# Attention with memory, then a gated feed-forward layer, on one core: another order of work around each full pair's values

## The chip, the cores and the metric

The kernel is one program on one core of a Trainium2 chip. Its time is the device time of one execution in microseconds (us). A run is repeated, and the median of the runs is what counts. One more execution is taken with the hardware profiler, and all rows below come from that one. The core has four engines that compute: TensorE (PE, with its weight loads shown as PEld), VectorE (DVE), ScalarE (ACT) and GpSimd (POOL). SyncE (SP) issues most of the transfers. Each engine works through its own list of instructions in the order in which the program has them.

## The reference

```python
# q, k, v: (B=4, H=8, S=576, D=64); M_prev: (4, 8, 64, 64); z_prev: (4, 8, 64); beta: (8,)
scores = scale * np.matmul(q, k.transpose(0, 1, 3, 2))        # scale = 1/8
scores = np.where(causal, -1000000000.0, scores)
a = np.exp(scores - scores.max(-1, keepdims=True))
a /= a.sum(-1, keepdims=True) + 1e-09
local = np.matmul(a, v)
q_p = np.where(q > 0, q, np.exp(q) - 1.0) + 1.0
mem_ret = np.einsum('bhsd,bhde->bhse', q_p, M_prev)
mem_norm = np.einsum('bhsd,bhd->bhs', q_p, z_prev)[..., None] + 1e-06
g = 1.0 / (1.0 + np.exp(-beta))[None, :, None, None]
x = g * mem_ret / mem_norm + (1 - g) * local                  # -> (2304 tokens, 512)
h = x @ w_in                                                  # w_in (512, 2048)
out = (h * (1.0 / (1.0 + np.exp(-1.702 * h)))) @ w_out        # w_out (2048, 512)
```

## The kernel before

The work falls into three stages. In the first, up to about 100 us, the weights `w_in` are decoded and the first batch's attention is done. In the second, up to about 400 us, come the other three batches: 12 pairs of heads, each a "full pair". In the third the rest of the first matrix product and then the second matrix product run without attention.

The first matrix product is cut into 8 chunks of 256 or 320 tokens and 16 blocks of 128 columns, which makes 128 products. Each is 12 matmuls into one PSUM bank named `pm` (float values are split in a high and a low part, so three matmuls for each of four slices). There are two such banks while attention runs. ACT copies a finished bank out as `hk` (`gate`, line 981 stores it), and only then can the bank take another product. In the second stage these products fill TensorE's time between the parts of a pair.

One full pair does the following:

- `first_group`: scores of the fourth block of 128 rows, for two heads (tiles `ps`, 128x512). DVE takes the row maxima with the mask (`max_unit`, line 634, one custom instruction and a read of its accumulator, which lands in `nm`), ACT takes the exponentials with their sums (`exp_unit`, line 640), DVE adds and inverts the sums (lines 720 and 721), POOL scales the rows (line 643), and DVE transposes them in blocks of 32 into `eT` (`a_blocks`, line 847).
- `second_group`: the same for the third, second and first block of rows, in four banks named `rows`. These are the banks in which the values of the pair before stood (`po`), so the group waits until those have been read.
- `early_values`: the scores of the next pair's last 64 rows (`s_tail`), then the first half of the values in four banks `po`: the memory's part (`qpt`, `mr`) and the keys from block 8 on. The second half (keys 0 to 7) stands in `values["next"]` and is taken up by the next pair's `first_group`, ahead of its own scores.
- `x_sums` reads the values: ACT copies them as the high part `xh`, DVE subtracts to get the low part `xl`.
- Beside it POOL, ACT and DVE make the next pair's query features (`plan_prep`: `qmt`, `qp`, `nrm`), and `decode` turns the raw words of `w_out` into floats: one scaling on ACT (line 1085, `r<-wraw`) and three integer operations on DVE (lines 1067 to 1070).

The order is written by slots. `at(slot, prio, fn)` puts a piece of work in a slot, and within a slot the lower priority number comes first. A full pair takes eight slots from its `k0`. After the pieces of a slot `step` fills up with matmuls of the first matrix product, until a pace of 2.3 us of counted TensorE time per slot is reached:

```python
fill["debt"] += next(v for t, v in PACE if s < t) - (state["pe"] - t0)
while fill["debt"] > 0:
    r = next(fill["gen"], None)
```

A scheduler then orders each engine's list. `tc.add_manual_dep(..., NOSYNC, ...)` forces an order within one engine without a wait on the chip. With SYNC it is a wait.

## Time and profile before

| | us |
|---|---|
| median of 3 runs | 656.95 (653.60 to 657.05) |
| the profiled execution | 652.16 |
| its span, first to last instruction | 650.4 |
| PE busy | 562.4 |
| DVE busy | 424.6 |
| ACT busy | 341.4 |
| POOL busy | 250.4 |

The busy times are sums over stages that differ. The second stage is the one in which TensorE pauses. The rows below show that stage and one full pair of it, from the end of one pair's scores of the fourth rows to the end of the next pair's.

### The profile page before, as it was taken

What the parts mean: (1) busy time and instruction counts of PE and PEld (TensorE: products, weight loads), DVE (VectorE), ACT (ScalarE), POOL (GpSimd) and SP (SyncE); (2) the same over time, 40 slices, a digit from 0 to 9 for tenths busy, and PEclk for the clock granted to TensorE, in tenths of its full rate; (3) what the DMA queues carried; (4) which work ended last, traced back from release to release, by engine and by line L of the source; (5) the groups of instructions that cost most, each with busy time, mean ns of one, the idle gap of its engine ahead of it and who ended that gap; (6) DMA issues with size and microseconds to landing.
All of it is one profiled execution on the core that took longest, in us unless ns stands there. A gap on an engine that the chain in (4) does not pass through costs nothing. (4 is left out here: it accounts for less than half of the span.)

```text
span 650.4 us, 17377 instructions
## 1 busy us (share of the span) xinstructions
PE 562.4 (86%) x6984; PEld 497.4 (76%) x6984; DVE 424.6 (65%) x993; ACT 341.4 (52%) x816; POOL 250.4 (38%) x326
## 2 busy tenths in 40 slices
PE   5799898778768777787777877999999999999997
PEld 3377676556657666576665667999999999999997
DVE  5887875556656646476465473676649778856964
ACT  6687874334344344253353452475576775586442
POOL 4766586346356343463454533221041310230000
PEclk9599999888888897899989998999999999999999
DMA  7975445545544454454533435532274560472002
GB/s 253 372 254 188 126 141 162 177 126 160 177 129 150 150 167 129 134 171 156 176 131 131 133 110 182 204 111 94 92 253 120 177 190 15 135 242 96 24 1 74
DMA packets 48737, 97.74 MB, mean 150 GB/s; under 512 B 5520, under 2 KB 33424, under 8 KB 48656
## 3 DMA queue, kind: packets, MB, share of 16 engines
q1 hardware_dynamic: 42416, 74.60, 35.3%
q0 software_dynamic: 6240, 22.02, 10.9%
q8 instruction: 55, 0.90, 0.6%
q14 instruction: 26, 0.21, 0.1%
HBM read 73.01 MB, written 23.59 MB: 149 GB/s over the span
## 5 line engine op out<-in xcount | busy, mean ns | idle before, releaser
L141 PE MATMUL pm<-xh,wi 128*128 128x320 f32 (+1 forms) x1024 | 222.9, 312 | 43.0 <-ACT hk L160 39.2
L141 PEld LDWEIGHTS pm<-xh,wi 128*128 128x128 f32 x1024 | 171.6, 197 | 66.9 <-ACT hk L160 44.8
L1235 PE MATMUL acc<-oh,wo 128*128 128x384 f32 x672 | 169.7, 337 | 0.0
L141 PE MATMUL pm<-xl,wi 128*128 128x256 f32 (+1 forms) x512 | 154.9, 303 | 0.0
L1235 PEld LDWEIGHTS acc<-oh,wo 128*128 128x128 f32 x672 | 121.9, 188 | 0.0
L1235 PE MATMUL acc<-ol,wo 128*128 128x384 f32 x336 | 111.2, 337 | 0.0
L168 DVE TENSOR_TENSOR ol<-g,oh 128x768 fp32r<-128x768 f32 x84 | 79.8, 955 | 42.8 <-ACT oh L160 42.6
L643 POOL TENSOR_SCALAR a<-a,sm,g 128x512 f32<-128x512 f32 (+3 forms) x112 | 74.6, 676 | 69.9 <-DVE sm L721 59.3
L141 PEld LDWEIGHTS pm<-xl,wi 128*128 128x128 f32 x512 | 101.2, 198 | 0.0
L160 ACT ACTIVATE oh<-g 128x768 fp32r<-128x768 f32 x84 | 69.8, 841 | 46.7 <-PE acc L1235 35.8
L1178 POOL DMA_DIRECT2D g<-gd x48 | 34.8, 726 | 115.0 <-DVE ol L168 90.6
L141 PE MATMUL po<-eT,vr 32*64 32x64 f32 (+4 forms) x3072 | 52.9, 257 | 23.5 <-issue 23.5
L160 ACT ACTIVATE hk<-pm 128x256 f32<-128x256 f32 (+1 forms) x113 | 44.8, 410 | 49.8 <-PE pm L141 27.2
L141 PEld LDWEIGHTS po<-eT,vr 32*64 32x64 f32 x3072 | 47.2, 135 | 26.8 <-issue 26.7
L1235 PEld LDWEIGHTS acc<-ol,wo 128*128 128x128 f32 x336 | 62.9, 188 | 0.0
L640 ACT ACTIVATE a<-rows,nm 128x256 f32<-128x256 f32 (+1 forms) x72 | 33.2, 471 | 33.3 <-DVE nm L634 33.3
L847 DVE STREAM_TRANSPOSE eT<-a 128x1024 f32<-128x1024 f32 (+3 forms) x48 | 40.4, 842 | 14.1 <-POOL a L643 12.2
L640 ACT ACTIVATE a<-ps,nm 128x512 f32<-128x512 f32 (+1 forms) x40 | 26.5, 666 | 42.9 <-DVE nm L634 42.9
L1184 ACT ACTIVATE g<-g 128x768 f32<-128x768 f32 x48 | 39.6, 840 | 14.6 <-DMA g<-gd 14.3
L634 DVE CUSTOM_DVE_ANT_0 ps<-ps,mask 128x512 f32<-128x512 f32 (+3 forms) x72 | 38.2, 558 | 13.1 <-PE ps L141 12.1
L168 DVE TENSOR_TENSOR g<-g,g 128x768 f32<-128x768 f32 x48 | 45.4, 952 | 1.4 <-ACT g L1184 1.4
L168 POOL TENSOR_TENSOR qp<-qp,nrm 128x576 f32<-128x576 f32 (+1 forms) x16 | 17.2, 1072 | 75.0 <-DVE nrm L588 74.7
(146 smaller groups left out, 763.8 us busy)
## 6 DMA issues: line engine op xcount, KB each, us to landing
g<-gd POOLq DMA_DIRECT2D x48, 384.0 KB, 4.6
vr<-in_vt_dram SPq DMA_DIRECT2D x24, 576.0 KB, 4.2
gd<-hk SPq DMA_DIRECT2D x64, 160.0 KB, 2.7
kqf<-in_kq_dram SPq DMA_DIRECT2D x12, 768.0 KB, 4.7
wraw<-in_w_in_dram SPq DMA_DIRECT2D x16, 512.0 KB, 5.5
gd<-hk SPq DMA_DIRECT2D x64, 128.0 KB, 2.1
wraw<-in_w_out_dram SPq DMA_DIRECT2D x10, 512.0 KB, 3.5
qr<-in_qt_dram SPq DMA_DIRECT2D x12, 288.0 KB, 3.1
```

Of the source, the lines that this page charges most:

```text
L141: x = nc.tensor.matmul(out, l, r, start=start, stop=stop)
L160: return nc.scalar.activation(out=dst, in_=src, func=AF.Copy, **kw)
L168: return (nc.vector if eng == "V" else nc.gpsimd).tensor_tensor(out=dst, in0=a, in1=b, op=op)
L634: nc.vector.tensor_tensor_reduce(out=ps, in0=ps, in1=mk, op0=ALU.add, op1=ALU.min, scale=-0.125, scalar=1e38 if j == 0 else nm[:, j - 1:j] ...
L640: return nc.scalar.activation(out=a, in_=ps, func=AF.Exp, scale=-1.0, bias=nm, accum_out=sm)
L643: return (nc.vector if eng == "V" else nc.gpsimd).tensor_scalar(out=a, in0=a, scalar1=r, scalar2=gcol, op0=ALU.mult, op1=ALU.mult)
L847: x = nc.vector.transpose(out=blocks()[:, :4 * i + 4, i:9 - i:8 - 2 * i].rearrange("p k h n -> p h k n"), in_=U["a", i].rearrange("p h (k ...
L1178: x = nc.gpsimd.dma_start(t, gd[4 * kh + p][:, :, t0:t0 + QN].rearrange("i p t -> p i t"))
L1184: x = nc.scalar.activation(out=t, in_=t, func=AF.Gelu_apprx_sigmoid)
L1235: nc.tensor.matmul(acc[b, j][:, :QN], W[2 * p + kk][:, WPART[i], sp, 128 * j:128 * j + 128], mv[:, kk], start=first and p + kk == 0 and sp ...
```

## The change

- The second group stands one slot earlier, and one whole product of the first matrix product is put directly ahead of it and one directly behind it (`feed`, which goes on until a product is finished).
- One whole product is put behind the first half of the values, before the next pair's `first_group` takes the second half.
- `x_sums` leaves the subtractions to a new piece `x_rests`, one slot later and ordered behind the fourth rows' maxima of the next pair.
- In the second group the exponentials of the first and second rows get priorities behind the copies `hk`, those of the third rows stay ahead. `behind_hk` orders these exponentials and the pieces of `plan_prep` behind the last `hk`.
- `decode` loads seven slots later, so that its scaling and its integer operations fall under the values, and the integer operations are ordered behind the latest maxima instead of behind `xl`.

```diff
+    def behind_hk(x):
+        if "turn" in late_ps:
+            tc.add_manual_dep(x.ins, state["hk"], NOSYNC, reason="not yet")
...
             for x in xs:
                 tc.add_manual_dep(x.ins, state["exp"], NOSYNC, reason="not yet")
+                behind_hk(x)
...
+            if i < 2:
+                behind_hk(x)
             U["exp", h, i] = state["exp"] = state["late A"] = x.ins.name
...
-            for xl, src, xh in subs:
-                values["po"] = values["x"] = tt("V", xl, src, xh, ALU.subtract).ins.name
+
+        def x_rests():
+            for xl, src, xh in U["subs"]:
+                x = tt("V", xl, src, xh, ALU.subtract)
+                tc.add_manual_dep(x.ins, state["max"], NOSYNC, reason="not yet")
+                values["po"] = values["x"] = x.ins.name
             late_ps.pop("po").close()
...
-        at(k0 + 4, 20, second_group)
-        for i, k in ((3, 0), (2, 4), (1, 4), (0, 4)):
+        at(k0 + 3, 18, lambda: feed(1.0, True))
+        at(k0 + 3, 20, second_group)
+        at(k0 + 3, 22, lambda: feed(1.0, True))
+        for i, k in ((3, 0), (2, 3), (1, 3), (0, 3)):
+            x = k0 + k + 1
             for h in range(2):
                 at(k0 + k + 1, 13 - i, lambda h=h, i=i: max_unit(h, i))
-                at(k0 + k + 1, 28 - i, lambda h=h, i=i: exp_unit(h, i))
-                at(k0 + k + 2, 13 - i, lambda h=h, i=i: scale_unit(h, i))
+                at(x, (30, 29, 26, 25)[i], lambda h=h, i=i: exp_unit(h, i))
+                at(x + 1, 13 - i, lambda h=h, i=i: scale_unit(h, i))
...
         at(k0 + 7, 40, early_values)
+        at(k0 + 7, 99, lambda: feed(1.0, True))
...
+        at(k0 + 9, 15, x_rests)
...
+    def feed(us, whole=False):
+        end, done = state["pe"] + us, not whole
+        while (state["pe"] < end or not done) and fill["gen"] is not None:
+            gates = state["gates"]
+            r = next(fill["gen"], None)
+            if r is None:
+                fill["gen"] = None
+            done = not whole or state["gates"] > gates
+            if r:
+                return
...
+        def bits():
+            tc.add_manual_dep(bit_ops(raw, words, words).ins, last_max[0], NOSYNC, reason="not yet")
...
-        at(K0[MB * NP + 2 + i] - 4, 58, lambda i=i: decode(i))
+        at(K0[MB * NP + 2 + i] + 3, 58, lambda i=i: decode(i))
```

The order that results is shown for the pair of the rows below (the ninth full pair). First TensorE between the two halves of the values. `po` are the values, the rows with 64x32 are the last of the first half, those with 64x160 the first of the second. Before:

```order
L141 MATMUL po<-eT,vr 64x32 x4
L141 MATMUL po<-eT,vr 64x64
L141 MATMUL po<-eT,vr 64x32 x6
L141 MATMUL po<-eT,vr 64x160
L141 MATMUL po<-eT,vr 64x128
L141 MATMUL po<-eT,vr 64x160
L141 MATMUL po<-eT,vr 64x128 x2
```

Now:

```order
L141 MATMUL po<-eT,vr 64x32 x4
L141 MATMUL po<-eT,vr 64x64
L141 MATMUL po<-eT,vr 64x32 x6
L141 MATMUL pm<-xh,wi_524 128x320 x2
L141 MATMUL pm<-xl,wi_524 128x320
L141 MATMUL pm<-xh,wi_524 128x320 x2
L141 MATMUL pm<-xl,wi_524 128x320
L141 MATMUL pm<-xh,wi_524 128x320 x2
L141 MATMUL pm<-xl,wi_524 128x320
L141 MATMUL pm<-xh,wi_524 128x320 x2
L141 MATMUL pm<-xl,wi_524 128x320
L141 MATMUL po<-eT,vr 64x160
```

One product of 12 matmuls (block 524 of the program's names) has moved in between the halves.

Next DVE from the values to the scores' maxima. `eT<-at` is the transposition of the last 64 rows, `ps` with 128x512 are the fourth rows' maxima, `xl` the subtractions, `r` the integer operations of the decoding. Before:

```order
L856 STREAM_TRANSPOSE eT<-at 128x2x32
L168 TENSOR_TENSOR xl<-po,xh 128x256 x2
L168 TENSOR_TENSOR xl<-po,xh 64x64 x2
L855 STREAM_TRANSPOSE eT<-at 128x16x32
L586 TENSOR_REDUCE nrm<-qmt 128x9
L588 RECIPROCAL nrm<-nrm 128x9
L634 ISA ps,nm<-ps,mask 128x512
L634 ISA nm 128x1
L634 ISA ps,nm<-ps,mask 128x512
L634 ISA nm 128x1
```

Now:

```order
L1102 TENSOR_SCALAR r<-r 128x512
L1103 SCALAR_TENSOR_TENSOR r<-wraw,r 128x512
L1105 SCALAR_TENSOR_TENSOR r<-wraw,r 128x512
L869 STREAM_TRANSPOSE eT<-at 128x2x32
L642 ISA ps,nm<-ps,mask 128x512
L642 ISA nm 128x1
L642 ISA ps,nm<-ps,mask 128x512
L642 ISA nm 128x1
L168 TENSOR_TENSOR xl<-po,xh 128x256 x2
L168 TENSOR_TENSOR xl<-po,xh 64x64 x2
L868 STREAM_TRANSPOSE eT<-at 128x16x32
L592 TENSOR_REDUCE nrm<-qmt 128x9
```

The integer operations stood behind the maxima and now stand ahead of them. The subtractions, the long transposition and `nrm` stood ahead of the maxima and now stand behind.

A little further on DVE, from `nrm` to the second group's maxima (`rows`), the changed kernel has two orders. In six of the twelve pairs, the ninth among them, the transposition of the fourth rows (128x2x16x32) stands ahead of the second group's maxima, as it did before:

```order
L594 RECIPROCAL nrm<-nrm 128x9
L733 RECIPROCAL sm<-sm 128x2
L612 STREAM_TRANSPOSE qpt_4648<-qp 128x9x2x32
L860 STREAM_TRANSPOSE eT<-a_4531 128x2x16x32
L642 ISA rows,nm<-rows,mask 128x384
L642 ISA nm 128x1
L642 ISA rows,nm<-rows,mask 128x384
L642 ISA nm 128x1
```

In the six others, the eighth pair among them, it stands behind two or more of them:

```order
L594 RECIPROCAL nrm<-nrm 128x9
L733 RECIPROCAL sm<-sm 128x2
L612 STREAM_TRANSPOSE qpt_4264<-qp 128x9x2x32
L642 ISA rows,nm<-rows,mask 128x384
L642 ISA nm 128x1
L642 ISA rows,nm<-rows,mask 128x384
L642 ISA nm 128x1
L860 STREAM_TRANSPOSE eT<-a_4148 128x2x16x32
```

Nothing but the place of that transposition, and in some pairs that of `qpt`, differs between the two.

Last ACT from the fourth rows' exponentials (128x512) to the copies behind the second group. Before:

```order
L640 ACTIVATE a_4515,sum_162<-ps,nm 128x512 x2
L1085 ACTIVATE r<-wraw 128x512
L160 ACTIVATE mr<-mr,g 128x2x64 x2
L160 ACTIVATE hk<-pm 128x320 x3
L640 ACTIVATE a_4636,sum_163<-rows,nm 128x384 x2
L640 ACTIVATE a_4639,sum_164<-rows,nm 128x256
L640 ACTIVATE a_4639,sum_165<-rows,nm 128x128
L640 ACTIVATE a_4639,sum_164<-rows,nm 128x256
L640 ACTIVATE a_4639,sum_165<-rows,nm 128x128
L557 ACTIVATE qmt<-qr 128x9x64
L160 ACTIVATE hk<-pm 128x320 x2
L563 ACTIVATE qmt<-qmt 128x9x64
```

Now, from the copy of the product between the halves on:

```order
L160 ACTIVATE hk<-pm 128x320
L1120 ACTIVATE r<-wraw 128x512
L160 ACTIVATE xh<-po 128x256 x2
L160 ACTIVATE xh<-po 64x64 x2
L649 ACTIVATE a_4531,sum_162<-ps,nm 128x512 x2
L160 ACTIVATE mr<-mr,g 128x2x64 x2
L160 ACTIVATE hk<-pm 128x320 x2
L649 ACTIVATE a_4631,sum_163<-rows,nm 128x384 x2
L160 ACTIVATE hk<-pm 128x320
L649 ACTIVATE a_4643,sum_164<-rows,nm 128x256 x2
L649 ACTIVATE a_4643,sum_165<-rows,nm 128x128 x2
L160 ACTIVATE hk<-pm 128x320
```

The scaling `r<-wraw` has moved ahead of `xh`, and one copy `hk` now stands between the exponentials with 128x384 and the four smaller ones, where it stood behind all six and behind `qmt`.

## Rows read from the trace of the kernel before

**Rows 1.** Busy time by stage: PE, PEld, DVE, ACT, POOL, then clock, DMA share, GB/s

```profile
100.60:400.60 300.00, 231.21 (x4759) 190.35 (x4758) 173.44 (x525) 121.84 (x401) 139.08 (x177) 0.94 0.48 150
400.60:470.30 69.70, 69.70 (x501) 69.70 (x500) 47.58 (x93) 38.34 (x71) 13.38 (x10) 0.98 0.38 131
```

**Rows 2.** What TensorE waited for from 95 to 402 us: total, times, longest

```profile
PE pm L141 <- ACT hk L160: 39.2, 21, 3.8
PE po L141 <- issue: 23.5, 15, 2.7
```

**Rows 3.** Timeline of TensorE, one pair: start, us, what, idle before

```profile
289.57 0.77 PE L141 MATMUL ps<-kqf 64*64 64x256 f32 x8
...
290.79 3.00 PE L141 MATMUL po<-eT,vr 32*64 32x64 f32 x197
294.83 1.14 PE L141 MATMUL po<-eT,vr 32*64 32x128 f32 x59 [1.05 <-issue]
295.90 1.09 PE L141 MATMUL ps<-kqf 64*64 64x512 f32 x8
...
303.57 0.55 PE L141 MATMUL pm<-xh,wi 128*128 128x320 f32 x2 [2.85 <-ACT hk L160]
...
305.52 1.52 PE L141 MATMUL rows<-kqf 64*64 64x384 f32 x24
...
312.25 0.50 PE L141 MATMUL pm<-xh,wi 128*128 128x256 f32 x2 [1.49 <-ACT hk L160]
...
319.49 1.41 PE L141 MATMUL po<-eT,vr 32*64 32x128 f32 x79 [1.40 <-issue]
320.83 1.09 PE L141 MATMUL ps<-kqf 64*64 64x512 f32 x8
```

**Rows 4.** Timeline of ACT in the same pair

```profile
296.01 0.99 ACT L160 ACTIVATE xh<-po 128x256 fp32r<-128x256 f32 x4 [3.27 <-PE po L141]
300.61 0.69 ACT L640 ACTIVATE a<-ps,nm 128x512 f32<-128x512 f32 x1 [3.61 <-DVE nm L634]
...
301.95 0.66 ACT L1085 ACTIVATE r<-wraw 128x512 f32<-128x512 f32 x1
...
303.09 0.74 ACT L160 ACTIVATE hk<-pm 128x320 f32<-128x320 f32 x2
...
307.78 0.58 ACT L640 ACTIVATE a<-rows,nm 128x384 f32<-128x384 f32 x1 [1.67 <-DVE nm L634]
...
311.75 0.77 ACT L160 ACTIVATE hk<-pm 128x320 f32<-128x320 f32 x2
```

**Rows 5.** Timeline of DVE in the same pair

```profile
297.03 1.12 DVE L168 TENSOR_TENSOR xl<-po,xh 128x256 fp32r<-128x256 f32 x4 [0.70 <-ACT xh L160]
298.18 0.71 DVE L855 STREAM_TRANSPOSE eT<-at 128x512 f32<-128x512 f32 x1
...
299.82 0.70 DVE L634 CUSTOM_DVE_ANT_0 ps<-ps,mask 128x512 f32<-128x512 f32 x1
...
302.64 0.43 DVE L1067 TENSOR_SCALAR r<-r 128x512 int32<-128x512 int32 x1 [0.19 <-ACT r L1085]
...
303.83 1.14 DVE L1070 SCALAR_TENSOR_TENSOR r<-wraw,r 128x512 int32<-128x512 int32 x1
305.65 1.25 DVE L847 STREAM_TRANSPOSE eT<-a 128x1024 f32<-128x1024 f32 x1 [0.68 <-POOL a L643]
...
311.41 0.97 DVE L847 STREAM_TRANSPOSE eT<-a 128x768 f32<-128x768 f32 x1
```

**Rows 6.** Timeline of POOL in the same pair

```profile
299.87 1.15 POOL L168 TENSOR_TENSOR qp<-qp,nrm 128x576 f32<-128x576 f32 x1 [5.72 <-DVE nrm L588]
...
303.58 2.03 POOL L643 TENSOR_SCALAR a<-a,sm,g 128x512 f32<-128x512 f32 x2
309.91 1.30 POOL L643 TENSOR_SCALAR a<-a,sm,g 128x384 f32<-128x384 f32 x2 [4.29 <-DVE sm L721]
```

**Rows 7.** The page's DMA queues: the queue that fetches instructions

```profile
q8 instruction: 55, 0.90, 0.6%
```

More of the change, by code (lines that the diff above doesn't have):

```diff
@@ L85, in tile_attention_memory_moe @@
     events = {}
-    state = {"slot": -8, "pe": 0.0, "seq": 0, "sum": 0, "bank": 0}
+    state = {"slot": -8, "pe": 0.0, "seq": 0, "sum": 0, "bank": 0, "gates": 0}
     def bank(name):
@@ L616, in plan_prep @@
         else:
-            times = (6, 7, 8, 9, 10, 11)
-            at(s0 + 10, 53, mplain)
+            times = (7, 7, 8, 9, 10, 11)
+            at(s0 + 11, 53, mplain)
             at(s0 + 12, 53, qblocks)
@@ L629, in plan_prep @@
             at(K0[p + 1] - 1, 61, lambda: load_m(p + 1))
+    last_max = [None]
     def softmax_max(pieces):
@@ L633, in softmax_max @@
         for j, (ps, n, mk) in enumerate(pieces):
-            nc.vector.tensor_tensor_reduce(
+            x = nc.vector.tensor_tensor_reduce(
                 out=ps, in0=ps, in1=mk, op0=ALU.add, op1=ALU.min, scale=-0.125,
                 scalar=1e38 if j == 0 else nm[:, j - 1:j], accum_out=nm[:, j:j + 1])
+            last_max[0] = x.ins.name
         return nm[:, len(pieces) - 1:len(pieces)]
@@ L701, in max_unit @@
             U["nm", h, i] = softmax_max([(U["ps", h, i][:, :n], n, mask[:, 512 - n:])])
+            state["max"] = last_max[0]
         def exp_unit(h, i):
@@ L715, in exp_unit @@
             used(U.get(("in", h, i), U["ps", h, i]), x)
+            if i < 2:
+                behind_hk(x)
             U["exp", h, i] = state["exp"] = state["late A"] = x.ins.name
@@ L830, in turn_over @@
         early.close()
+        late_ps["turn"] = True
         late_ps["a"] = pool(attn, "ps_a", 2, space=PSUM, side="right", reuse_waits="tile")
@@ L897, in x_sums @@
         def x_sums():
-            subs = []
+            subs = U["subs"] = []
             for ch in range(2):
@@ L955, in plan_full @@
         at(k0, 20, first_group)
-        at(k0 + 4, 20, second_group)
-        for i, k in ((3, 0), (2, 4), (1, 4), (0, 4)):
+        at(k0 + 3, 18, lambda: feed(1.0, True))
[3 more added lines that the diff above has]
+            x = k0 + k + 1
             for h in range(2):
                 at(k0 + k + 1, 13 - i, lambda h=h, i=i: max_unit(h, i))
-                at(k0 + k + 1, 28 - i, lambda h=h, i=i: exp_unit(h, i))
-                at(k0 + k + 2, 13 - i, lambda h=h, i=i: scale_unit(h, i))
-            at(k0 + k + 1, 91 - i, lambda i=i: inv_unit(i))
+                at(x, (30, 29, 26, 25)[i], lambda h=h, i=i: exp_unit(h, i))
+                at(x + 1, 13 - i, lambda h=h, i=i: scale_unit(h, i))
+            at(x, 91 - i, lambda i=i: inv_unit(i))
             at(k0 + k + 3, 13 - i, lambda i=i: a_blocks(i))
         at(k0 + 7, 40, early_values)
+        at(k0 + 7, 99, lambda: feed(1.0, True))
         if p + 1 == len(pairs):
@@ L974, in gate @@
         t0 = b * S + a0
+        state["gates"] += 1
         def keep():
@@ L1086, in scale @@
             tc.add_manual_dep(x.ins, state["exp"], NOSYNC, reason="not yet")
+            behind_hk(x)
         at(state["slot"] + 5, 56, scale)
-        at(state["slot"] + 5, 57, lambda: behind_x(bit_ops(raw, words, words)))
+        def bits():
+            tc.add_manual_dep(bit_ops(raw, words, words).ins, last_max[0], NOSYNC, reason="not yet")
+        at(state["slot"] + 5, 57, bits)
     for i in range(2 * len(HERE)):
-        at(K0[MB * NP + 2 + i] - 4, 58, lambda i=i: decode(i))
+        at(K0[MB * NP + 2 + i] + 3, 58, lambda i=i: decode(i))
     fill["gen"] = first_moe()
```

## The prediction

> **What bounds the kernel now.** I read the busy time by stage first. From 100.6 to 400.6 us the twelve full pairs run, 25.0 us each, and TensorE is busy for 231.2 of 300 us; in the stage behind, it is busy all of the time [rows 1]. The first matrix product is a fixed amount of work that fills TensorE there, and by the order the changed kernel leaves as many of its products for behind the attention as before. So TensorE time saved among the pairs shortens the whole, and at most about 68 us can be saved.
>
> Next, what TensorE waited for in that stage: 39.2 us on copies `hk` by ACT that free a product's bank, in 21 waits, and 23.5 us ahead of values' matmuls, in 15 waits that nothing else in the profile ends ("issue") [rows 2].
>
> Then one pair on the timelines. I count from 296.99 us, the end of its scores of the fourth rows, to 321.92, the end of the next pair's: 24.93 us [rows 3]. There are three pauses.
>
> A, 2.85 us. Two products run, the third waits for a bank. ACT's copies come only at +6.1 us, behind the exponentials, which wait for the maxima: DVE starts these at +2.8 us, since the subtractions, the long transposition and `nrm` stand ahead. Then come scaling of raw words and `mr`, 1.14 us [rows 3 to 5].
>
> B, 1.49 us. Two products behind the second group, the third waits for a copy that stands behind six exponentials and `qmt`, at +14.8 us [rows 3, 4].
>
> C, 1.40 us, within the values. The instruction queue moved 55 packets with 0.90 MB [rows 7], for about 14,000 TensorE instructions (matmuls and weight loads), so one packet holds about 254, which is 127 matmuls. The values' matmuls pass at 3.00 us for 197 [rows 3], 15 ns each, so 127 of them last 1.9 us. I read C as TensorE having used a packet up before the next has come, some 3.4 us after the packet before began to run.
>
> **The change part by part.** All times are from +0, durations from the rows.
>
> The decoding. ACT copies the product between the values' halves, then scales the raw words (0.66 us), both while the second half of the values runs (128 matmuls, 1.95 us, then 1.09 us of scores). The product ends at about -3.0, the scaling at -1.9, the three integer operations take 2.33 us [rows 5] and end at +0.5. Read off the other end, with a late copy, it is +1.4. I take +0.9. The cover is the values themselves, in which DVE was idle; what stays visible is up to 1 us ahead of the maxima. The raw words are asked for behind the fourth rows' exponentials, about +3, and used at about +18 of the same pair, so the load has some 15 us.
>
> A. The maxima start at +1.1, the first exponential 0.79 later (299.82 to 300.61) at +1.9, both end at +3.3, `mr` takes 0.5, and the two copies stand at +3.8 to +4.5 where they stood at +6.1 to +6.9. TensorE runs two products (1.87 us each, 303.57 - 2.85 - 296.99 over two) to +3.7, then the second group. That group needs the values' banks, and so the subtractions, which are now late: maxima end at +2.4, the subtractions (1.12) at +3.5. The group starts at about +3.8. Of 2.85 us, 0.3 stay; with 256-token products, which are shorter, up to 1.
>
> DVE behind. The long transposition and `nrm` took 1.64 us from start to the maxima (298.18 to 299.82), so they end at +5.2, the sums and inverses at +5.5. POOL multiplies by `nrm` (1.15) to +6.5 and scales the fourth rows (2.03) to +8.6 [rows 6]. The second group (1.46) ends at +5.3.
>
> Now the two orders on DVE differ. *Maxima first (six pairs):* they start at about +5.5, or up to +7.3 behind `qpt`; the 384-wide exponentials end at +7.2 to +9.0 and the copy behind them frees a bank at +7.6 to +9.4. The third product is wanted at +8.9, so B goes. But the fourth rows' transposition (1.25) then runs from +8.6 to +9.9, the last maxima and inverses to +10.5, POOL's 384-wide scaling (1.30) to +11.8, the transposition (0.97) to +12.8 [rows 5, 6]. This releases the first half of the values. TensorE has work to about +11.0, so 1.8 us of wait come in B's place. *Transposition first (six pairs):* it runs +8.6 to +9.85, the exponentials start 0.95 later (as 306.90 to 307.78), end at +11.95, the copy at +12.3. The third product waits 3.4 us, twice B. The scaling and transposition end at +14.4.
>
> From there: tail scores and values take 5.28 us without C (295.90 - 289.57 - 1.05 [rows 3]), 1.95 of it the second half, the product between the halves 1.87, the fourth rows' scores 1.09, together 8.2. The pair ends at +21.0 or +22.6 without C.
>
> C. A product between the halves puts 12 slow matmuls in about 115 quick ones: 1.7 + 1.87 us, about what a packet needs. A packet still lies whole within one half when it begins in the first 160 + 8 - 127 = 41 matmuls of the first, or the first 128 + 8 - 127 = 9 of the second: 50 of 127. So 5 of 12 pairs keep about 1.6, the others a few tenths, and two packets lie in one pair at times: 12 us in all where 23.5 stood. That is 1.0 per pair.
>
> The Trainium skill, "Runtime: NRT & Kernel Launch", section "Instruction fetch mechanics", says that instructions come in blocks of 256, ahead of use, and that crossing a block costs little that shows. The block's size agrees with 254. By its second half C would have another cause and stay, and the sum would be 11 us smaller. Against it speaks how C lies: always a packet's length into the quick matmuls.
>
> Sum: periods of 22.0 and 23.6 against 24.93, so 6 x 2.9 + 6 x 1.3 = 25 us. At the three batch ends the first product of the new batch needs the late subtractions: lost, 0 to 2 us each, I take 2 in all. The granted clock averages 0.94 in the stage [rows 1]: 12% of 300 us, 36 us, at the lower level of 1.2 GHz. Shorter pauses may give back 0 to 12 us; I take 4. The profiled execution took 652.16 us: 652 - 27 = 625. The median of the runs lies 4.8 above that execution, so I write 629.
>
> **The rivals.** *Everything better (0.15):* DVE runs ahead so far that all pairs go like the good six, and the clock stays up. 12 x 2.9 + 2 x 4 = 43 us: 609 on the profile's base, 613 for a median. For it: DVE is busy 173 of 300 us only. Against: POOL's chain of 1.15 and 2.03 us behind `nrm`.
>
> *C stays (0.10):* not a matter of fetching, or the packets lie badly. 629 + 11 = 640.
>
> *The wait only moves (0.17):* B and the wait for the values' first half grow as A shrinks, in all pairs as in the poor six, and the integer operations run late by another 0.9. Period 24.5; 0.4 x 12 = 5 us: 652. For it: in the poor six the transposition of the fourth rows ends at +9.85, and at 306.90, which is +9.9, before.
>
> *Slower (0.08):* the decoding under the values becomes the path. ACT works in order, so if the raw words or the copy ahead come late, `xh`, the maxima and the subtractions are late with them, and the values' banks block the second group. Every us by which the maxima start behind +2.8 (where they stood) goes into the period in full, and at +2.8 the period is about 25: two maxima of 0.70 and the subtractions end at +5.3, the group starts there, and all behind it is 1.5 later than above, in the poor order 25.1. At +4.5 it is 26.8, 12 x 1.9 = 23 us more: 680.
>
> **How the numbers follow.** The forecast has 0.50, with 617 to 643 as its own range. A measurement can't tell less than 0.5% here, 3.3 us, from no change: below 653.7 is faster, above 660.2 slower. The forecast, the first two rivals and over half of the third lie below: 0.84 faster. The rest of the third gives 0.09, the last 0.07. For 8 in 10 the range runs from 609 to 651.
>
> **What would show it.** Right: A's pause nearly gone; copies `hk` about 4 us behind the fourth rows' scores; waits "issue" near 12 us in sum; TensorE idle below 45 us in the stage; pairs ending sooner where the second group's maxima come first. Wrong: maxima that start at +2.5 or later; TensorE waiting for subtractions ahead of `rows`; a third product that waits over 3.5 us behind the second group in all pairs; or the last stage, busy throughout now, opening gaps.

## The result and the profile after

The changed kernel takes 626.62 us (median of 4 runs, 624.67 to 628.42), the kernel before 657.0 us beside it (4 runs, 653.6 to 662.56): a ratio of 0.953, with a 95% interval of 0.946 to 0.960. The forecast was 629. The profiled execution took 625.55 us for a span of 623.8, where 625 was forecast on the profile's own base.

The stages, cut at the first matmul of `rows` in the first full pair, at the end of the last values, and at the end of the first product. Columns as in [rows 1]: the stretch, its length, busy time of PE, PEld, DVE, ACT and POOL, then TensorE's granted clock.

```profile
102.50:368.70 266.20, 227.73 (x4774) 191.68 (x4774) 162.29 (x524) 124.75 (x403) 132.69 (x176) 0.96 0.54 166
368.70:442.60 73.90, 67.87 (x481) 66.94 (x482) 50.86 (x95) 37.12 (x69) 13.91 (x11) 0.98 0.37 129
```

Against [rows 1], the stage of the pairs is 33.8 us shorter: idle time of TensorE fell from 68.8 to 38.5 us, its busy time from 231.2 to 227.7. But the stage behind, in which TensorE was busy all of 69.7 us, now lasts 73.9 with 6.0 us idle. The start is 1.9 us longer as well. So the total came out as forecast with two errors against each other: the pairs gained more, and the last stage lost. The cut between the stages is not quite the same, either: 480 matmuls of the first product are left behind the attention where 498 were, so 18 more are done among the pairs.

What TensorE waited for from 95 to 369 us, which ends with the stage as in [rows 2] (total, times, longest):

```profile
PE ps L141 <- DVE sm L733: 13.8, 5, 4.6
PE pm L141 <- ACT hk L160: 10.7, 10, 3.0
PE po L141 <- issue: 6.9, 6, 2.1
PE ps L141 <- issue: 2.9, 1, 2.9
PE rows L141 <- DVE xl L168: 1.9, 3, 0.6
```

The copies `hk` went from 39.2 us in 21 waits to 10.7 in 10, the pauses "issue" of the values from 23.5 to 9.8 (6.9 ahead of `po`, 2.9 ahead of `ps`). New is a wait of the tail's scores, 13.8 us.

One pair of the kind "transposition first" on TensorE, the eleventh ([rows 3] shows the ninth of the kernel before), from the end of its fourth rows' scores (+0 is 322.75) to the next such scores:

```profile
321.66 1.09 PE L141 MATMUL ps<-kqf 64*64 64x512 f32 x8
...
325.70 1.53 PE L141 MATMUL rows<-kqf 64*64 64x384 f32 x24
...
333.14 0.50 PE L141 MATMUL pm<-xh,wi 128*128 128x256 f32 x2 [2.99 <-ACT hk L160]
...
338.11 0.77 PE L141 MATMUL ps<-kqf 64*64 64x256 f32 x8
...
339.33 1.88 PE L141 MATMUL po<-eT,vr 32*64 32x64 f32 x128
...
342.66 2.47 PE L141 MATMUL po<-eT,vr 32*64 32x160 f32 x128
345.05 1.09 PE L141 MATMUL ps<-kqf 64*64 64x512 f32 x8
```

The values now lie in two halves of 128 matmuls with a product from 341.14 to 342.66 between them, and neither half holds a pause. ACT in the same pair, beside [rows 4]:

```profile
323.59 0.69 ACT L649 ACTIVATE a<-ps,nm 128x512 f32<-128x512 f32 x1 [0.84 <-DVE nm L642]
...
325.52 0.67 ACT L160 ACTIVATE hk<-pm 128x256 f32<-128x256 f32 x2
331.58 0.58 ACT L649 ACTIVATE a<-rows,nm 128x384 f32<-128x384 f32 x1 [5.40 <-DVE nm L642]
...
332.71 0.38 ACT L160 ACTIVATE hk<-pm 128x256 f32<-128x256 f32 x1
```

DVE in the same pair, beside [rows 5]:

```profile
322.80 0.70 DVE L642 CUSTOM_DVE_ANT_0 ps<-ps,mask 128x512 f32<-128x512 f32 x1 [0.72 <-PE ps L141]
...
324.06 1.11 DVE L168 TENSOR_TENSOR xl<-po,xh 128x256 fp32r<-128x256 f32 x4
...
329.59 1.25 DVE L860 STREAM_TRANSPOSE eT<-a 128x1024 f32<-128x1024 f32 x1 [0.73 <-POOL a L652]
330.87 0.57 DVE L642 CUSTOM_DVE_ANT_0 rows<-rows,mask 128x384 f32<-128x384 f32 x1
...
343.81 0.43 DVE L1102 TENSOR_SCALAR r<-r 128x512 int32<-128x512 int32 x1 [2.14 <-ACT r L1120]
```

POOL in the same pair, beside [rows 6]:

```profile
326.90 1.15 POOL L168 TENSOR_TENSOR qp<-qp,nrm 128x576 f32<-128x576 f32 x1 [8.48 <-DVE sm L733]
```

The maxima start 0.05 us behind the scores, the integer operations of the decoding run under the values (343.81), the copies come at +2.8, where they stood at +6.1. The fourth rows' transposition ends at 330.84, the second group's maxima begin at 330.87, and the third product waits 2.99 us for the copy at 332.71. The queue that fetches instructions moved as many packets as in [rows 7].

Two tables are worked out from the records of the traces, one profiled execution of each kernel. The first is the mean of ten pairs of each kernel, the second to the eleventh, in us, from TensorE's matmuls alone: from the end of the fourth rows' scores to the start of `rows`; from the end of `rows` to the tail's scores; from there to the end of the next fourth rows' scores. The experiments are named by their sections below.

```
kernel                       scores->rows  rows  rows->tail  tail->scores   pair
before                          8.99       1.58     6.55        8.67       25.8
changed                         3.77       1.54     7.78        9.78       22.9
no split                        4.96       1.53     7.23        8.57       22.3
no split, maxima in front       5.03       1.53     6.41        8.58       21.5
maxima in front (with split)    3.77       1.55     7.25       10.30       22.9
no split, earlier group         2.82       1.53    10.54        8.66       23.6
both of these                   2.91       1.61     9.53        8.52       22.6
```

The last row is "no split, earlier group" with the maxima in front.

The second splits the stage of the pairs into TensorE's idle time, half of the time at the lower clock level, and the rest; the last column is idle time in the stage behind. Half, because work takes nearly twice as long there: in the pair above three matmuls of a 256-token product take 0.64 us at the lower level (at 334 to 337 us) and 0.34 at the upper. The table is bookkeeping: whether time at the lower level lengthens the whole by that half is another question, taken up under "Decoding back".

```
kernel                       stage   idle   time at 1.2 GHz   rest    idle behind
before                       300.0   68.8        37.5         212.4       0.0
changed                      266.1   38.5        23.9         215.7       6.0
no split                     262.7   39.8        25.6         210.1       0.0
no split, maxima in front    253.2   37.3        15.3         208.2       0.0
maxima in front              267.7   37.0        34.1         213.7       6.3
decoding back                294.2   52.6        54.6         214.3       2.2
```

### The profile page after: what moved, and what is told of

It is laid out like the page before. It is cut to its first block, busy times and chain, and to the rows that moved or that the text cites. A ratio compares the mean times of both kernels' runs of the same rounds, so it can differ in the third digit from the quotient of the medians.

```text
span 623.8 us, 17375 instructions
## 1 busy us (share of the span) xinstructions
PE 559.6 (90%) x6984; PEld 497.3 (80%) x6984; DVE 417.1 (67%) x993; ACT 343.1 (55%) x816; POOL 244.8 (39%) x326
## 4 chain that ended last, share of the span: by engine, by line
PE 33%; issue 10%; DVE 9%; POOL 4%; DMA 4%; ACT 3%; POOLq 0%; ACTq 0%; DVEq 0%
PE acc L1274 15%; PE pm L141 11%; PE po L141 5%; POOL g L1217 2%; DMA g<-gd 2%; DMA wraw<-in_w_out_dram 2%; PE ps L141 2%; POOL a L652 2%; DVE eT L860 1%; ACT a L649 1%; DVE ps L642 1%; DVE xl L168 1%; DVE rows L642 1%; DVE g L168 1%; DVE eT L868 1%
## 5 line engine op out<-in xcount | busy, mean ns | idle before, releaser
L141 PE MATMUL pm<-xh,wi 128*128 128x320 f32 (+1 forms) x1024 | 220.6, 309 | 19.9 <-ACT hk L160 16.2
L141 PEld LDWEIGHTS pm<-xh,wi 128*128 128x128 f32 x1024 | 169.5, 195 | 39.1 <-ACT hk L160 19.4
L141 PEld LDWEIGHTS pm<-xl,wi 128*128 128x128 f32 x512 | 99.9, 195 | 0.9 <-DVE xl L168 0.9
L652 POOL TENSOR_SCALAR a<-a,sm,g 128x512 f32<-128x512 f32 (+3 forms) x112 | 69.2, 629 | 44.5 <-DVE sm L733 34.0
L649 ACT ACTIVATE a<-rows,nm 128x256 f32<-128x256 f32 (+2 forms) x72 | 33.2, 473 | 45.2 <-DVE nm L642 33.4
L141 PE MATMUL ps<-kqf 64*64 64x512 f32 (+3 forms) x288 | 39.5, 547 | 20.1 <-DVE sm L733 13.8
L141 PEld LDWEIGHTS po<-eT,vr 32*64 32x64 f32 x3072 | 48.6, 136 | 10.2 <-issue 9.7
```

The costliest lines, as they stand in the source:

```text
L141: x = nc.tensor.matmul(out, l, r, start=start, stop=stop)
L649: return nc.scalar.activation(out=a, in_=ps, func=AF.Exp, scale=-1.0, bias=nm, accum_out=sm)
L652: return (nc.vector if eng == "V" else nc.gpsimd).tensor_scalar(out=a, in0=a, scalar1=r, scalar2=gcol, op0=ALU.mult, op1=ALU.mult)
```

## The experiments

Each time stands beside runs of the kernel before on the same chip; the ratios are to those, with 95% intervals.

**Without the product between the halves** ("no split").

```diff
-        at(k0 + 7, 99, lambda: feed(1.0, True))
```

> The changed kernel, but with no whole product between the two halves of the values; the number of products among the pairs stays the same. Theory (a pause in the values is TensorE out of fetched instructions): the pauses that nothing else ends come back, from about 10 us in sum to 20 to 24, nearly all of them visible: 636 to 640 us against 627. Rival 1 (the pauses have another cause, the product between the halves does nothing to them): about 10 us in sum as in the changed kernel, 625 to 629. Rival 2 (they come back, but are covered by the wait for the first half's transpositions, which is then shorter): 20 to 24 us in sum, but only 628 to 632.

616.93 us (615.99 to 619.23, 4 runs), ratio 0.943 (0.937 to 0.948). Waits of TensorE, 95 to 365 us:

```profile
PE po L141 <- issue: 20.0, 14, 3.5
PE ps L141 <- DVE sm L733: 11.5, 5, 5.1
PE pm L141 <- ACT hk L160: 6.9, 11, 1.1
```

All three expectations missed: the pauses of the values come back as the theory has it, 20.0 us where the changed kernel has 9.8, and still the time falls. TensorE's idle sum is the same, 39.8 and 38.5: what the split took from "issue" had gone into `hk` and the tail's scores. And the last stage has no pause. The comparison is not quite clean, since the order on DVE changes with it: the fourth rows' transposition stands first in eleven of the twelve pairs here and in seven of the changed kernel. A clean one follows below, "The same without the split".

**Subtractions back ahead of the maxima.**

```diff
-        def x_rests():
-            for xl, src, xh in U["subs"]:
-                x = tt("V", xl, src, xh, ALU.subtract)
-                tc.add_manual_dep(x.ins, state["max"], NOSYNC, reason="not yet")
...
+            for xl, src, xh in subs:
+                values["po"] = values["x"] = tt("V", xl, src, xh, ALU.subtract).ins.name
...
-        at(k0 + 9, 15, x_rests)
```

> The changed kernel, but with the subtractions xl back ahead of the fourth rows' maxima, as they stood before; by the order the long transposition and nrm go with them, so the maxima start at about +2.9 us again, and TensorE's order stays. Theory (the gain of pause A comes from the maxima standing first): copies hk come at +5.7 instead of +2.8, the third product waits about 0.7, the fourth rows' chain is late by up to 2 us: 11 pairs by 1.3 us, 638 to 644. Rival (it comes from the second group standing between the second and the third product, which covers the late copies; nrm is earlier by 1.4 us and POOL's chain no later than +0.3): 626 to 631.

643.35 us (639.83 to 643.87, 4 runs), ratio 0.981 (0.975 to 0.988): 17 us above the changed kernel. Waits for `hk` rise from 10.7 us to 24.5 within the pairs, and the first copies come at +5.0 to +5.5 us in most pairs, near the expected +5.7. The time lies in the theory's range: maxima first is worth what was said.

**Decoding back.**

```diff
-            tc.add_manual_dep(bit_ops(raw, words, words).ins, last_max[0], NOSYNC, reason="not yet")
+            behind_x(bit_ops(raw, words, words))
...
-        at(K0[MB * NP + 2 + i] + 3, 58, lambda i=i: decode(i))
+        at(K0[MB * NP + 2 + i] - 4, 58, lambda i=i: decode(i))
```

> The changed kernel, but with the decoding of w_out back at its old place, seven slots earlier, its integer operations on DVE behind nrm and ahead of the second group's maxima. Theory (DVE idles about 2 us there in a pair, waiting for POOL, so 2.3 us of integer operations nearly fit): 0 to 0.5 us in ten pairs, 627 to 633. Rival (they stand on the path to the second group's maxima): 2.3 us in ten pairs, 645 to 650.

646.4 us (641.82 to 647.4, 4 runs), ratio 0.986 (0.979 to 0.992): 20 us above, in the rival's range: the integer operations do stand on the path. The stretch of its pairs (the stage itself runs from 101.8 to 396.0 us):

```profile
100.00:394.00 294.00, 241.03 (x4713) 201.44 (x4716) 167.28 (x530) 126.22 (x406) 142.10 (x178) 0.91 0.48 154
```

Idle time is 14 us more than in the changed kernel, and busy time 13 more (241.0 against 227.7) at a clock of 0.91 against 0.96. The stage is 28 us longer by the second table. In that bookkeeping about half is the clock, with 54.6 us at the lower level where the changed kernel has 23.9. That the clock costs this much is not shown: two runs of this version, with a granted clock of 0.940 and 0.959 over the whole, took 646.24 and 646.57 us, where half of the time at the lower level would make 12 us between them. What the trace does show is the chain: the transposition `qpt` on DVE, behind which the second group's maxima stand, ends 7.2 us behind the fourth rows' scores in most pairs, 1.1 later than in the changed kernel, and from these scores to the tail's it is 14.1 us on average instead of 13.1.

**Exponentials ahead of the copies again.**

```diff
-        if "turn" in late_ps:
-            tc.add_manual_dep(x.ins, state["hk"], NOSYNC, reason="not yet")
+        return
...
-                at(x, (30, 29, 26, 25)[i], lambda h=h, i=i: exp_unit(h, i))
+                at(x, 28 - i, lambda h=h, i=i: exp_unit(h, i))
```

> The changed kernel, but with the second group's six exponentials and qmt ahead of the copy hk again, as they stood before. Theory (pause B is set by that copy): the third product behind the second group waits 2.2 us longer in all pairs that have three, 11 x 1 to 2.2 us: 638 to 650, and waits for copies by ACT go from 12 us to 25 to 35. Rival (the wait for the transpositions ahead of the first half takes over, so the third product has slack): 626 to 632, with the sum of TensorE's waits unchanged.

635.93 us (635.33 to 637.41, 4 runs), ratio 0.972 (0.965 to 0.979). Waits of TensorE, 95 to 390 us:

```profile
PE pm L141 <- ACT hk L160: 28.4, 13, 4.4
PE ps L141 <- DVE sm L732: 6.9, 2, 4.8
```

The order on ACT is worth 9 us by the medians, between the rival's range and the theory's. The waits are the theory's: `hk` waits of up to 4.4 us stand in 13 places where there were 10 and the longest was 3.0.

**The split alone**, put into the kernel before.

```diff
         at(k0 + 7, 40, early_values)
+        at(k0 + 7, 99, lambda: feed(1.0, True))
```

> The kernel before, with nothing but the product between the values' two halves. By the theory formed since (a pause taken out of the values only moves to the next wait, since the pair's period is set by the chain from the second group's rows over maxima, exponentials, scaling and transposition to the values): the waits 'issue' shrink from 23.5 to about 10 us, the waits for hk or sm grow by as much, and the time is 648 to 660, as before. By the prediction's own term the pauses' 11.5 us are gained: 641 to 647.

655.97 us (654.66 to 657.83, 10 runs), ratio 1.001 (0.999 to 1.004). Waits of TensorE, 95 to 402 us:

```profile
PE pm L141 <- ACT hk L160: 35.7, 17, 4.9
PE ps L141 <- DVE sm L721: 10.3, 2, 5.7
PE po L141 <- issue: 8.2, 10, 3.5
PE ps L141 <- issue: 2.2, 1, 2.2
```

"Issue" falls from 23.5 to 10.4 us and nothing is gained: the time lies in the theory's range, 648 to 660. The waits follow it only in part. The tail's scores now wait 10.3 us, but the waits for `hk` fell, and the idle sum did fall, by 10.5 us to 58.3. Against that stand 54.6 us instead of 37.5 at the lower clock, 18 more matmuls of the first product among the pairs, and 3.6 us of pauses in the last stage. How much each of them took is not shown; the ten runs, at granted clocks of 0.940 to 0.952, are not shorter where the clock is higher.

**The decoding alone**, moved in the kernel before.

```diff
-        at(state["slot"] + 5, 57, lambda: behind_x(bit_ops(raw, words, words)))
+        def bits():
+            tc.add_manual_dep(bit_ops(raw, words, words).ins, last_max[0], NOSYNC, reason="not yet")
+
+        at(state["slot"] + 5, 57, bits)
...
-        at(K0[MB * NP + 2 + i] - 4, 58, lambda i=i: decode(i))
+        at(K0[MB * NP + 2 + i] + 3, 58, lambda i=i: decode(i))
```

> The kernel before, with the decoding of the raw words alone moved under the values. By the theory that DVE's integer operations (2.33 us) and ACT's scaling stood in the chain of each pair, and that each us there counts nearly in full and holds the clock down: 9 pairs by 1 to 2 us, 635 to 648. Rival: they filled DVE's wait for POOL's scaling, and what the decoding was worth in the changed kernel (20 us when put back) comes only with the maxima first: 651 to 658.

646.94 us (644.75 to 651.25, 10 runs), before 652.19 on that chip: ratio 0.992 (0.989 to 0.996). The median lies in the theory's range, but the kernel before was 3 us quicker there than beside the other runs, so the gain is 5 us: more than the rival's nothing, and less than the 7 to 20 that the theory stood for. Alone the move is worth a quarter of what it is worth beside the maxima.

**Second group's maxima in front in all pairs**, with the split.

```diff
+            if i == 3:
+                tc.add_manual_dep(x.ins, state["max"], NOSYNC, reason="not yet")
...
-            at(k0 + k + 3, 13 - i, lambda i=i: a_blocks(i))
+            at(k0 + k + 3 + (i == 3), 14 if i == 3 else 13 - i, lambda i=i: a_blocks(i))
```

> The changed kernel with the transposition of the fourth rows behind the second group's maxima in all pairs on DVE (the prediction's 'maxima first' in all twelve pairs). By the prediction: pairs with the transposition first are 1.3 to 2.6 us longer (23.6 and 22.0 by the working, 24.0 and 21.4 measured), so 12 x 2 or so fewer among the six: 611 to 619. Rival: their waits are of the same size in either order, the pairs in question differ for another reason (they hold 384-token neighbours, more products and more fetching), and the time stays within 623 to 630.

628.78 us (625.5 to 631.24, 4 runs), ratio 0.958 (0.952 to 0.964): no gain, as the rival had it. Waits of TensorE, 95 to 371 us:

```profile
PE ps L141 <- DVE sm L733: 10.7, 4, 4.8
PE po L141 <- issue: 10.6, 7, 4.8
PE ps L141 <- issue: 4.3, 4, 2.5
PE pm L141 <- ACT hk L160: 3.8, 8, 0.7
PE ps L141 <- DVE eT L860: 3.4, 1, 3.4
```

The third product no longer waits (the longest `hk` wait is 0.7 us), so the edit did what it says; other waits took the place. Telling is the time from the fourth rows' scores to the tail's scores: 12.3 to 12.7 us in each pair from the second to the eleventh, and in nine of the first eleven pairs TensorE stands idle, by 0.4 to 4.8 us, just ahead of the tail's scores. So that part has a length of its own, set by something else than TensorE's work in it.

What sets it can be read from the trace. The eighth pair, whose fourth rows' scores end at 255.05 us and whose `rows` are done at 260.22:

```profile
260.38 0.78 DVE L612 STREAM_TRANSPOSE qpt<-qp 128x576 f32<-128x576 f32 x1 [1.25 <-POOL qp L168]
261.20 0.57 DVE L642 CUSTOM_DVE_ANT_0 rows<-rows,mask 128x384 f32<-128x384 f32 x1
...
266.50 0.98 DVE L860 STREAM_TRANSPOSE eT<-a 128x768 f32<-128x768 f32 x1 [0.90 <-POOL a L652]
...
267.74 0.77 PE L141 MATMUL ps<-kqf 64*64 64x256 f32 x8 [2.05 <-DVE sm L733]
```

The second group's maxima do not start when `rows` are there but behind `qpt`, which waits for POOL's multiplication by `nrm`. In nine of the ten pairs from the second to the eleventh they start at +6.15, whether `rows` came at +2.58 or at +5.08. At the other end, the third rows' transposition is done at 267.48 and the tail's scores start 0.26 us later. `early_values` puts these scores in one group with the first half of the values, ahead of them, and by `group` the first matmul of the group waits for all that the values need, the third and fourth rows' transpositions among it. In each of the nine pairs with a pause, one of the two ends 0.10 to 0.26 us ahead of the tail's scores. (The profile puts the wait down to `sm` of line 733, a small instruction of the same engine just behind it.) So the chain runs through DVE's list: maxima, subtractions, `nrm`, POOL's multiplication, `qpt`, the second group's maxima, and over ACT and POOL to the transposition. Moving what stands in it moved this part: from 13.1 us in the changed kernel to 14.1 with the decoding back, 14.4 with the subtractions back and 14.6 with the exponentials back. POOL's multiplication and `qpt` themselves were not moved. The tail's scores need no transposed rows themselves; what it would give to take them out of that group was not tried.

**The same without the split** ("no split, maxima in front").

> The changed kernel without the product between the halves, and with the transposition of the fourth rows behind the second group's maxima in all pairs (there the transposition stands first in ten). If the order on DVE is worth 2.6 us in a pair whatever else is done, the time falls to 595 to 605. Rival: with the rows a product later, the transposition ends before the rows are there, so its order costs nothing, and putting it last makes the values' first half wait for it: 615 to 630.

607.27 us (605.9 to 614.12, 4 runs), ratio 0.928 (0.921 to 0.935), the fastest version, on the same chip as the one above. Its stages:

```profile
102.30:355.50 253.20, 215.93 (x4756) 182.78 (x4755) 172.32 (x525) 123.54 (x400) 138.19 (x177) 0.97 0.55 176
355.50:426.00 70.50, 70.50 (x500) 70.50 (x501) 47.35 (x93) 38.44 (x71) 13.37 (x10) 0.96 0.38 130
```

And its waits, 95 to 356 us:

```profile
PE po L141 <- issue: 21.8, 15, 2.7
PE ps L141 <- DVE sm L733: 11.0, 5, 4.2
...
PE pm L141 <- ACT hk L160: 0.4, 1, 0.4
```

The time lies between the two expectations. Nearly the whole of the kernel before's pauses "issue" stands here (21.8 of 23.5 us), and the kernel is 48 us faster than that one. The copies have ceased to matter, 0.4 us. This is the clean comparison of the split, with the maxima in front in all twelve pairs either way and beside the same runs: 628.8 with it, 607.3 without.

**Second group a slot earlier**, without the split.

```diff
-        at(k0 + 3, 20, second_group)
+        s = 3 if p == MB * NP else 2
+        at(k0 + s, 20, second_group)
...
-        for i, k in ((3, 0), (2, 3), (1, 3), (0, 3)):
+        for i, k in ((3, 0), (2, s), (1, s), (0, s)):
```

> The changed kernel without the product between the halves, with the second group of rows asked for one slot earlier in all pairs but the first, so that one product fewer stands ahead of the rows and one more behind them. By the chain theory the rows start about 1.5 us earlier (as soon as the subtractions are done, some +3 us), and all behind them with them: 12 pairs by about 1 us, 600 to 610. Rival: the chain isn't the limit any more without the split; TensorE's own work and the fetch pauses (20 us) are, and the time is that without the split alone, 614 to 620; TensorE then waits for the subtractions or for hk instead.

630.31 us (629.03 to 632.35, 4 runs), ratio 0.962 (0.956 to 0.968): 13 us slower than without the split alone, against both expectations. `rows` do start 2.1 us earlier (first table), but the tail's scores come 3.3 us later behind them.

```profile
PE po L141 <- issue: 24.7, 13, 4.9
PE pm L141 <- ACT hk L160: 23.1, 17, 2.3
```

In eight pairs of this version the fourth rows' transposition stood between two pairs of the second group's maxima, so the next run put the maxima in front.

**Earlier group and maxima in front.**

> Without the product between the halves, the second group asked for one slot earlier, and the fourth rows' transposition behind the second group's maxima in all pairs. Theory: the earlier group was slower only because the transposition of the fourth rows, waiting for POOL's scaling, came between two pairs of maxima on DVE; with the maxima in front the waits for hk (23 us) go, and the rows start 2 us earlier than with the later group: 590 to 606. Rival: the rows a slot earlier leave TensorE one product less to run under the maxima and exponentials ahead of them, so hk copies are late in any order, or nothing is left to gain since TensorE's work and its fetch pauses (22 us) fill the pair: 606 to 625.

623.88 us (620.94 to 626.57, 4 runs), ratio 0.958 (0.953 to 0.963). Beside their own runs of the kernel before, the two lie at 0.962 and 0.958, so that order brings back little if anything, and the version stays 17 us behind the one with the later group. Waits, 95 to 370 us:

```profile
PE po L141 <- issue: 22.5, 13, 3.8
PE pm L141 <- ACT hk L160: 13.5, 14, 2.1
```

The rival had it: with 1.5 products less ahead of `rows` (1.45 on average against 2.95) and as many more behind (4.67 against 3.17), the products wait for `hk`. The early `rows` buy little for it, since their maxima still start at +6.15, behind `qpt`, in eight of the ten pairs. And in eight of the ten the transposition was done 0.6 to 6.2 us ahead of the tail's scores, with no idle time just ahead of them: what comes late there is TensorE itself, with the products and their waits.

**Last pair's values whole**, else the changed kernel.

```diff
-        at(k0 + 7, 99, lambda: feed(1.0, True))
+        if p + 1 < len(pairs):
+            at(k0 + 7, 99, lambda: feed(1.0, True))
```

> The changed kernel with the values of the last pair in one piece (the product between the halves only in the pairs ahead of it). If the pauses that the last stage opened (6 us in the changed kernel, none without the split) come from the last pair's split, which brings the products behind it and so their copies out of step with the expert weights' decoding: the last stage is busy throughout and the time is 620 to 624. Rival: they come from the 18 products that the split moved ahead in all pairs (480 instead of 498 left), and stay: 625 to 629.

621.66 us (613.18 to 624.35, 4 runs), ratio 0.950 (0.943 to 0.957). The median's 5 us are within the intervals' overlap with the changed kernel; the trace decides. Its pairs and its last stage:

```profile
101.00:369.00 268.00, 227.22 (x4756) 190.13 (x4757) 162.47 (x525) 123.73 (x401) 133.42 (x177) 0.95 0.53 166
369.00:438.50 69.50, 69.50 (x499) 69.50 (x500) 48.02 (x93) 38.23 (x71) 13.36 (x10) 0.98 0.38 132
```

TensorE is busy throughout the last stage again, 69.5 us where the changed kernel has 73.9, and 498 matmuls are left behind the attention again: the 18 that were missing (matmuls, not products) are the last pair's alone. In the changed kernel the longest pause there, on TensorE's timeline:

```profile
398.38 0.59 PE L141 MATMUL pm<-xh,wi 128*128 128x256 f32 x2 [3.37 <-ACT hk L160]
```

Its copy stands on ACT behind a scaling of expert weights that waited for DVE, and behind a load of an activation table (the second and last of the execution):

```profile
395.26 0.63 ACT L1189 ACTIVATE ws<-wraw 128x512 f32<-128x512 f32 x1 [3.74 <-DVE wo L168]
395.92 1.28 ACT L1223 ACT_TABLE_LOAD   x1
397.21 0.84 ACT L1223 ACTIVATE g<-g 128x768 f32<-128x768 f32 x1
397.96 0.36 ACT L160 ACTIVATE hk<-pm 128x256 f32<-128x256 f32 x1
```

That the last pair's split brings these pauses is shown. That it does so because, with 18 matmuls between its halves, the products behind run out of step with that decoding, is my reading.

## Why the prediction came out, and where its steps failed

**Maxima first, and A.** Right, and somewhat better. The copies come at +2.8 us, not +3.8 to +4.5, since the decoding was through before the scores (maxima at +0.05, not +1.1), and `rows` start at +2.95, not +3.8. The first part of the pair fell from 8.99 to 3.77 us on average. Undoing the order costs 17 us.

**The decoding.** That it would be covered was right, but the term was mis-sized: the sum gave its old place no price of its own. Put back it costs 20 us. Moved alone it gains 5. In the kernel before it stood, as I read it, in the shade of late maxima; with the maxima early it stands in the way and delays `qpt` by 1.1 us. Parts like these don't add.

**C, the fetching.** The size of what remains was near, 9.8 us for a forecast of 12. The step that failed is the next: that this saving, 1.0 us a pair, goes into the period. It does not: the split alone gives nothing (1.001, 0.999 to 1.004), taking it out speeds the changed kernel up by 10 us by the medians, and with the maxima in front by 21. The working counted the product between the halves as work that TensorE has to do anyway. But it put that work on the path from the tail's scores to the next fourth rows' scores. With the maxima in front in all pairs, this path takes 10.30 us with the split and 8.58 without, while the other part, from the fourth rows' scores to the tail's, shrinks by only 0.4, from 13.0 to 12.6 us, for having one product less. There TensorE waits for the chain over DVE and POOL that the section on the maxima in front shows, and a product costs little.

The sum's own terms say as much. In the better order it lets the transposition release the values at +12.8 and adds 8.2 us, the product's 1.87 among them. Without the split TensorE has one product more ahead of the values, to about +12.9 instead of +11.0, which hardly moves the release, and behind it stand 6.4 us (5.28 + 1.09) and C's 2.0 (23.5 over 12): 21.2, where the forecast with the split is 22.0. Part of the loss is the last stage's: with the last pair whole, the profiled execution is 4.3 us shorter, though the runs spread too far to settle the size.

The reading of C itself holds. Numbering TensorE's records in the trace (matmuls, weight loads and some 60 instructions of its sequencer) from zero, all 55 pauses of over 0.7 us from start to start between two matmuls of values among the pairs, in the kernel before (15), the changed one (6), no split (13), the split alone (6) and the fastest (15), end at an instruction whose number leaves 193 when divided by 256, though the pairs run at other times in each. And each of the 55 ends 1.2 to 1.6 us after a packet of 16,384 bytes has landed on the queue that fetches instructions. The Trainium skill, "Runtime: NRT & Kernel Launch", section "Instruction fetch mechanics", has the 256 right; that crossing a block hardly shows does not hold here, with 23.5 us in the kernel before. By that rule the rival "C stays" would have given 640.

**The two orders on DVE.** By the trace the maxima come first in five pairs (2, 3, 4, 6 and 8) and the transposition in seven, not in six each. The periods are near: from the second pair to the eleventh, 21.4 us on average in the first order (22.0 forecast) and 24.3 in the second (23.6), with a third product that waits 2.99 us in the pair shown (3.4). One reading in the working is off without weight: from 306.90 to 307.78 it is 0.88 us, not 0.95. The cause that I gave for the difference was not the whole: with the maxima in front in all pairs, the time is the same (628.8). Without the split the order does pay, 617 to 607.

**The clock.** It was forecast to give back 4 us. The time at the lower level fell from 37.5 to 23.9 us, which counted at half is 6.8. That the total gained this is not shown: the profiled execution has the highest granted clock of the four runs, 0.978 over the whole, and the run with the lowest, 0.959, took 2.9 us longer, where this count would make it 12.

**The last stage.** That it would open gaps was among the signs of being wrong, and it opened 6.0 us of pauses: a step missing from the sum. The last pair's split brings them, as the run without it shows in its trace. The premise that as many products are left behind the attention failed there too, by 18 matmuls.

So the 629 is right for the parts that carry it (maxima, copies, decoding), which brought more than counted, while the split, credited with 12 us, cost time. That it agrees with the measured time to under 3 us is luck: the errors cancelled.

Of the rivals, the 609 to 613 of "everything better" are near what the chip does without the split and with the maxima in front in all pairs: 607 us, with the pauses of C in place. "The wait only moves" is true of one part of the change, the split, not of the whole. "Slower by the decoding" did not come.

## What to carry to other kernels

A pause on the bottleneck engine is worth its length only where nothing else is waiting at the same time; before filling it with work, find where in the period that engine already waits for a chain of other engines, and leave the filler there. When work is moved, count the path that it is moved onto as well as the engine's total. And test the parts of a change one by one: here the version without one of them beats the whole by 19 us when the order on DVE is set to match.

## What the hardware showed that was not expected

The same idle time can go with quite different clocks. With the group earlier, TensorE was idle for 53.4 us among the pairs and ran 18.6 us at the lower level; with the decoding put back it was idle for 52.6 us and ran 54.6 us at it. So the sum of idle time does not tell the clock; what does, no run here settles. Nor does the clock tell the time. Runs of one program differ in granted clock by some 0.02, and in time by less than half of the time at the lower level would make: two runs of "Decoding back" by 0.3 us instead of 12, two of the fastest version (0.953 and 0.974) by 8.2 instead of 13.

The pauses from fetching fall on the same instruction numbers in the traces of different versions: in the kernel before, no split and the fastest, on numbers 1985, 5057, 7617, 8385, 9153 and 10177 among others, 0.7 to 3.75 us each. The pairs run at other times in each of the three, up to 46 us apart at the end.
